# Block 0 of an adaLN transformer layer: three banks for exponentials, q and k sums as undivided products, gates' dots in the start's task list

## Chip, core and metric

One core of one Trainium2 chip. The metric is the device time of one execution in microseconds; of several runs the median is given. Before: 2514.73 us, median of 3 runs (2514.54 to 2520.65).

## What is computed

One transformer layer over 2048 rows of 576, with 32 heads of 18 and an MLP of 4608, conditioned on one vector `c`:

```python
mod = (silu(c) @ w_mod).reshape(1, 6, 1, 576)
sa, ca, ga, sb, cb, gb = (mod[:, i] for i in range(6))
h = layernorm(x) * (1 + ca) + sa
q, k, v = heads(h @ wqkv)                    # 32 heads of 18
x = x + ga * (softmax(q @ k.T * 18**-0.5) @ v) @ wo
h = layernorm(x) * (1 + cb) + sb
x = x + gb * (silu(h @ w1) @ w2)
```

All arrays are float32. Sums over the model's 576 columns are taken in three passes over a high and a low part of each operand (`PASS`: 14 products for 4 full and one folded group of 128 rows).

## The kernel before

**Stages.** The start (`start_tasks`) normalises all rows, transposes them into `hTh` and `hTl` (high and low part), takes the sums of k and q for the first columns and of all values, and stores them in DRAM (`kscr`, `qscr`, `vscr`). Attention then runs over 4 blocks of 512 query rows with 8 quads of 4 heads each. In block 0 the rest of the q and k sums is filled in between; in blocks 1 to 3 the output projection and the MLP of the block before are the filling, and block 3's MLP stands at the end.

**A slot of attention.** `slot_a` takes scores of queries against 512 keys (54 rows of the array, names `psa`) and VectorE their maximum (`mx`, `L670`). 38 slots later `slot_b` takes the same scores transposed, with the maxima in two further rows (56 rows of the array, `psb`), and ScalarE their exponential into `pt` (`L727`). Two heads sit in rows 0 to 63 and 64 to 127 of the array, so two score products run side by side: one pair is one psa and one psb product. When the four exponentials of a key tile are there, `pv` takes its values' run (`psv<-pt,vt`, `L762`): four heads in four groups of 32 columns. After 16 key tiles `out_b` transposes the quad's output (`pso`) and divides it. `max_b` transposes the maxima (`pst`) and writes them into rows of `qt` by DMA.

**Order.** TensorE's order is written at build time. For the start, `Start` plays a list of tasks with costs, dependencies, priorities and rings of buffers. For attention, a loop asks a model of VectorE and ScalarE (`Plan`, with a ring of banks for each PSUM pool) whether scores (`s`), a values' run (`v`) or filling (`f`) comes next. `Filler` holds the filling in order. The other engines' order is the scheduler's, except in the start's task list. An instruction that is recorded after the start can be drawn forward into it: the gates' loads are.

**PSUM.** Eight banks: `psB` 2 (scores for exponentials, `b`), `psF` 2 (sums, `f`), `psV` 1 (values, `v`), `psA` 3 (scores for maxima, and small transposes, `a`). `open_mlp`, called when the q and k sums are done, gives `psF` 3 and `psA` 2 for the rest.

**q and k sums in block 0** (`add_qk`, `qk_pair`). Twelve pairs of 512 columns. A pair takes both `psF` banks; `Pair.step` issues two products of 64 rows side by side, one for each bank, 28 steps in all; at half time the banks change their halves, behind an empty ScalarE instruction (`change`, `L470`) that the next products wait for. A product of 64 rows is in the same form of the array as the scores.

**Gates.** `mod_load` loads a column piece of `w_mod` (`wmt<-in_wcol`, `L491`), takes its dot with `sbc` on VectorE (`dot`, `L487`) and scales the identity by it (`dg`); `mod_piece` spreads it over the rows (`psm`). There are ten pieces, called from the filling of block 0. The start's task list has ten dots of its own (`wcl`, for the second modulation).

**Next weights.** `qk_load` loads a step's weights on ScalarE's queue (`raw<-in_wqkv`, `L512`), copies the high part on ScalarE (`wqh`, `L517`) and takes the low part on GpSimd (`L522`). Step 0's load stands in the start's task list.

Of the kernel before, what the change touches and what calls it, by code (L numbers as in the profile page):

```python
# [18 lines left out]
P = 128  # L19
# [6 lines left out]
KT = 5  # L26
# [23 lines left out]
XTB = 7  # L50
ETB = 3
# [14 lines left out]
NG = len(GR)  # L66
G2 = [range(i, i + 3) for i in range(0, 24, 3)]
# [7 lines left out]
EARLY_SLOTS = 16  # L75
KEEP = 6
NEAR = 500
LOADED = 900
STAND = 0
# [102 lines left out]
class Start:  # L182
# [3 lines left out]
    RATE = 300e3  # L186
# [16 lines left out]
    def ready(self, t):  # L203

        at = 0.0
        for d in t.deps:
            if d.end is None:
                return None
            at = max(at, d.end + (2.0 if d.eng == "D" else 0.0) + (self.LAG.get((d.eng, t.eng), 0.08) if d.eng != t.eng else 0.0) + t.lag)
# [12 lines left out]

    def run(self):
# [3 lines left out]
        while todo:  # L227
# [14 lines left out]
            for e, (_, t) in best.items():  # L242
# [10 lines left out]
                for k in t.free:  # L253
                    k.left -= 1
                    k.at = max(k.at, t.end + (2.0 if e == "D" else 0.0))
# [74 lines left out]
def tile_adaln_block(ctx: ExitStack, tc: tile.TileContext, x, wqkv, wo, w1, w2, c, wfirst, wcol, out):  # L330
# [9 lines left out]
    psF = ps0.enter_context(tc.tile_pool(name="psF1", bufs=2, space=PSUM))  # L340
# [76 lines left out]

    def bank_need():
# [70 lines left out]
    def mod_load(m, t):  # L489
        w = wqp.tile([P, D], F32, tag="wmt", name="wmt", bufs=2)  # L490
        nc.sync.dma_start(w, wcol[2 + m, :, t, :])  # L491
# [39 lines left out]
    def qk_load(which, m):  # L531
        raw = raw_load(qk_src(which, m), KT * P, nc.scalar)
# [3 lines left out]
    def qk_pair(which, m, ns, w, part):  # L536
        if part == 0:
            def ops(g, i):
                kt, a, b = PASS[i]
                return w[b][:, kt, :], (hTl if a else hTh)[:, kt, ns[g] * 512:(ns[g] + 1) * 512]  # L540
# [35 lines left out]
    state = {"now": 0, "p": 0, "k": 0, "tail": False, "tail2": False}  # L576
# [3 lines left out]
    def add_qk(steps):  # L580
        def load(i):
            which, m, _ = steps[i]
            fill.add(0, lambda: qk_w.update({i: qk_load(which, m)}))

        for i, (which, m, pairs) in enumerate(steps):
            for ns in pairs:
                names = [("qkx"[which], m, n) for n in ns]
                for p in range(NG):
                    fill.add(MMC * len(GR[p]), lambda i=i, which=which, m=m, ns=ns, p=p: qk_pair(which, m, ns, qk_w[i], p), name=names, need={0: pair_need, NG // 2: half_need}.get(p))
                    if ns == pairs[0] and p == 0 and i + 1 < len(steps):  # L590
                        load(i + 1)
                    if i >= MI and p in (NG // 2, NG - 1) and mods:
# [118 lines left out]
    def slot_b(s, j):  # L711
# [12 lines left out]
        ps = psB.tile([P, 512], F32, tag="b", name="psb", bufs=2)  # L724
# [69 lines left out]
    def open_mlp():  # L794
        nonlocal psF, psA
# [6 lines left out]
        plan.ring("f", 3)  # L802
        plan.ring("a", 2)
# [246 lines left out]
    def start_tasks(st):  # L1050
        S0 = Start({"b": 2, "f": 2, "v": 1, "a": 3, "xt": XTB, "wm": KT, "et": ETB, "vst": VSB, "qk": QKB, "raw": 2, "wq": 2})
# [78 lines left out]
        def T(g, kt):  # L1130
            d["T", g, kt] = psB.tile([P, 512], F32, tag="b", name="psT", bufs=2)
# [55 lines left out]
        def single(deps, ops, w, prio, key, free=()):  # L1187

            count[0] += 1
            ring = "v" if count[0] % 3 == 0 else "f"  # L1190
# [15 lines left out]
        def pair(deps, ops, w, n, prio, key, ring):  # L1206

            kb = tok(ring, 2)
            tasks = []

            def part(i):
                if i == 0:
                    ps = [(psF if ring == "f" else psB).tile([P, 512], F32, tag=ring, name="ps" + key[0], bufs=2)[:, :w] for _ in range(2)]
# [4 lines left out]
            for i in range(n):  # L1218
# [3 lines left out]
                tasks.append(add("P", (0.231 if w == 512 else 0.133) * 28 / n, lambda i=i: part(i), list(deps) + dep, prio, take=kb if i == 0 else ()))  # L1222
# [123 lines left out]
        for s in range(LEAD):  # L1346
# [6 lines left out]
            gate = h[3, KT - 1] if s >= EARLY_SLOTS else []  # L1353
# [10 lines left out]
        for n in range(2 * KT):  # L1364
# [10 lines left out]
        kr = tok("raw")  # L1375
        which, m, _ = steps[0]
        t = dma(328e3, lambda: d.update(rawn=raw_load(qk_src(which, m), KT * P, nc.sync)), prio=11, take=kr)
        kw = tok("wq")
        t = add("A", 0.74, lambda: d.update(whn=hi_part(d["rawn"])), [t], 11, take=kw)
        add("G", 1.54, lambda: qk_w.update({0: (d["whn"], lo_part(d["rawn"], d["whn"]))}), [t], 11, free=kr)  # L1380
# [12 lines left out]
    plan.ring("f", 2)  # L1393
    plan.ring("a", 3)
    plan.ring("b", 2)
# [23 lines left out]
    while now < 2 * (total + LEAD) or pend or later:  # L1419
# [17 lines left out]
        elif not mp:  # L1437

            if scores and ahead < AHEAD:
# [94 lines left out]
```

## Time and profile before

| | us |
|---|---|
| runs | 2520.65, 2514.54, 2514.73 |
| profiled execution, and its span | 2518.77, 2516.9 |
| first transpose on TensorE | 25.81 |
| first score product for a maximum | 63.72 |
| first exponential | 175.32 |
| last product of q and k sums | 564.6 |
| first output copy of block 0, and the last | 229.9, 613.1 |
| TensorE busy in 176 to 566 us | 385.15 of 390.00 |
| VectorE, ScalarE, GpSimd there | 312.88, 272.71, 10.94 |

Times of single instructions are from the span's start. A matmul's end is modelled, so TensorE's busy time also covers part of a wait; distances from one start to the next tell its pace. "PEld" is the weight load of a product, "SPq" and "ACTq" the issue of a DMA from SyncE's and ScalarE's queue, "ACTq L470" the empty instruction of `change`.

### The profile page before, as it was taken

The page shows a single profiled execution, that of the slowest core. Times are in us where ns is not written, and L with a number is a line of the kernel's source. Part 1 is how long each engine was busy: PE and PEld are TensorE (multiplying, and loading weights), DVE is VectorE, ACT ScalarE, POOL GpSimd, SP SyncE. Part 2 cuts the span into 40 slices and gives each one's busy share as a digit, 9 for nine tenths or more (in the row PEclk, how much of TensorE's full clock was granted, in tenths as well). Part 3 has the DMA queues.
Part 4 walks back from the last instruction along what each step waited for, and adds up shares of the span by engine and source line. Part 5 has one row for each costly group of instructions (what it writes and reads, how often), then busy time and mean ns, then how long its engine had stood idle before and what let it go on. Part 6 is the DMA issues. An engine that isn't in the chain of part 4 may idle for free.

```text
span 2516.9 us, 51969 instructions
## 1 busy us (share of the span) xinstructions
PE 2422.2 (96%) x20528; PEld 1617.7 (64%) x20528; DVE 1783.0 (71%) x3180; ACT 1498.0 (60%) x2712; POOL 577.1 (23%) x729
## 2 busy tenths in 40 slices
PE   4989999998999999999999999999999999999999
PEld 3874444542556666666666666666666666678988
DVE  6867878887786777777877777777877777324333
ACT  3326776776566666666576766666666666642121
POOL 3300000003375566654211111111211111110000
PEclk9999999999899999999999999999999999999999
DMA  7653233235265555554443433334543334226563
GB/s 244 200 170 120 93 107 102 88 111 180 78 202 173 166 170 189 191 162 162 160 145 125 145 119 135 121 123 131 181 146 126 126 134 142 102 95 235 171 222 122
DMA packets 159397, 372.07 MB, mean 148 GB/s; under 512 B 17754, under 2 KB 55034, under 8 KB 159154
## 3 DMA queue, kind: packets, MB, share of 16 engines
q1 hardware_dynamic: 153906, 366.12, 43.9%
q8 instruction: 163, 2.67, 0.4%
q10 hardware_dynamic: 5248, 2.62, 0.4%
q14 instruction: 80, 0.66, 0.1%
HBM read 282.35 MB, written 85.80 MB: 146 GB/s over the span
## 4 chain that ended last, share of the span: by engine, by line
PE 86%; DVE 7%; ACT 2%; DMA 2%; issue 1%; POOL 1%; SPq 0%; ACTq 0%; DVEq 0%; POOLq 0%
PE ps L459 26%; PE psv L762 18%; PE psa L668 14%; PE ps L453 9%; PE psb L725 9%; PE psqk L459 3%; DVE mx L670 3%; PE psp L459 1%; PE psv L459 1%; ACT pt L727 1%; PE pso L775 1%; PE psv L1199 1%; PE psqk L1199 1%; PE psp L453 1%; DVE st L368 1%
## 5 line engine op out<-in xcount | busy, mean ns | idle before, releaser
L670 DVE TENSOR_REDUCE mx<-psa 128x1 f32<-128x512 f32 x2048 | 1346.3, 687 | 387.4 <-PE psb L725 256.8
L727 ACT ACTIVATE pt<-psb 128x512 f32<-128x512 f32 x2048 | 1169.6, 597 | 569.9 <-PE psb L725 397.4
L725 PE MATMUL psb<-qt,kt 56*128 56x512 f32 x2048 | 817.2, 433 | 12.3 <-DMA qt<-mt 5.9
L668 PE MATMUL psa<-kt,qt 54*128 54x512 f32 x2048 | 780.2, 421 | 27.8 <-DVE mx L670 21.3
L668 PEld LDWEIGHTS psa<-kt,qt 54*128 54x128 f32 x2048 | 348.8, 185 | 393.1 <-DVE mx L670 247.3
L762 PE MATMUL psv<-pt,vt 128*32 128x512 f32 x4096 | 534.6, 606 | 0.8 <-DMA vt<-vscr 0.8
L459 PE MATMUL ps<-w2t,g 64*128 64x288 f32 x4992 | 418.1, 294 | 0.1
L459 PEld LDWEIGHTS ps<-w2t,g 64*128 64x128 f32 x4992 | 387.1, 185 | 35.1 <-issue 10.6
L725 PEld LDWEIGHTS psb<-qt,kt 56*128 56x128 f32 x2048 | 352.6, 185 | 78.9 <-ACT pt L727 58.4
L459 PE MATMUL ps<-hh,w1t 64*128 64x512 f32 x2160 | 386.2, 395 | 0.9 <-POOL hh L401 0.8
L459 PEld LDWEIGHTS ps<-hh,w1t 64*128 64x128 f32 x2160 | 221.7, 186 | 57.4 <-issue 10.6
L978 POOL TENSOR_TENSOR g<-etmp,g 128x512 fp32r<-128x512 f32 x108 | 138.9, 1302 | 405.8 <-ACT g L977 362.7
L883 POOL TENSOR_TENSOR x<-x,gt 128x288 f32<-128x288 f32 x116 | 92.7, 800 | 483.1 <-ACT gt L882 473.1
L762 PEld LDWEIGHTS psv<-pt,vt 128*32 128x32 f32 x4096 | 93.1, 108 | 171.4 <-issue 164.6
L459 PE MATMUL ps<-hl,w1t 64*128 64x512 f32 x864 | 186.7, 393 | 1.0 <-POOL hl L399 1.0
L879 DVE TENSOR_TENSOR x<-ps,x 128x288 f32<-128x288 f32 x184 | 84.0, 456 | 122.6 <-PE ps L453 71.5
L453 PE MATMUL ps<-w2t,g 128*128 128x288 f32 x960 | 130.6, 295 | 1.7 <-ACT g L977 0.9
L453 PEld LDWEIGHTS ps<-w2t,g 128*128 128x128 f32 x960 | 128.6, 188 | 3.3 <-ACT g L977 1.2
L974 ACT ACTIVATE eq<-ps 128x512 f32<-128x512 f32 x36 | 21.5, 598 | 146.4 <-PE ps L453 146.4
L453 PE MATMUL ps<-hh,w1t 128*128 128x512 f32 x360 | 106.9, 390 | 0.5 <-DVE hh L401 0.5
L522 POOL TENSOR_TENSOR wql<-raw,wqh 128x640 fp32r<-128x640 f32 x13 | 21.3, 1640 | 366.8 <-ACT wqh L517 340.0
L459 PEld LDWEIGHTS ps<-hl,w1t 64*128 64x128 f32 x864 | 94.0, 186 | 17.5 <-POOL hl L399 2.5
(136 smaller groups left out, 2085.5 us busy)
## 6 DMA issues: line engine op xcount, KB each, us to landing
w1t<-w1s SPq DMA_DIRECT2D x108, 640.0 KB
w2t<-w2s SPq DMA_DIRECT2D x108, 576.0 KB
kt<-kscr SPq DMA_DIRECT2D x512, 108.0 KB
w1s<-w1t SPq DMA_DIRECT2D x36, 640.0 KB
w2s<-w2t SPq DMA_DIRECT2D x36, 576.0 KB
vt<-vscr SPq DMA_DIRECT2D x32, 608.0 KB
qt<-qscr SPq DMA_DIRECT2D x128, 108.0 KB
raw<-in_w SPq DMA_DIRECT2D x72, 160.0 KB
```

The lines of the kernel that those rows point to most:

```text
L368: nc.vector.bn_stats(st6[:, j, :], src[:, j * HH:(j + 1) * HH])
L453: mm(self.ps[late], lhsT=lhsT, rhs=rhs, start=(i == 0), stop=(i == self.n - 1))
L459: done = mm(self.ps[g], lhsT=lhsT[rows], rhs=rhs[rows], start=(s == 0), stop=(s == 2 * self.n - 1))
L668: mm(ps, lhsT=t["q"][64 * j:64 * j + 54, hp, stt * P:(stt + 1) * P], rhs=t["k", kc, hp][64 * j:64 * j + 54, :], start=True, stop=True)
L670: return lambda: nc.vector.tensor_reduce(t["mx"][:, 2 * j + hp, stt, kc:kc + 1], ps, axis=AX.X, op=ALU.max)
L725: mm(ps, lhsT=t["k", kt // 4, hp][64 * e:64 * e + 56, kt % 4 * P:(kt % 4 + 1) * P], rhs=t["q"][64 * e:64 * e + 56, hp, :], start=True, sto ...
L727: nc.scalar.activation(t["P"][kt, hp][:, e, :], ps, AF.Exp, scale=SCALE)
L762: mm(t["ps"][32 * h:32 * h + 32, :], lhsT=t["v"][:, c0:c0 + 32], rhs=t["P"][kt, h // 2][:, h % 2, :], start=(kt == 0), stop=(kt == NKT - 1 ...
L879: nc.vector.tensor_add(c["x1"][j][:, hs], ps, c["x1"][j][:, hs])
L883: nc.gpsimd.tensor_add(c["x1"][j][:, hs], c["x1"][j][:, hs], t)
L978: (nc.vector if last else nc.gpsimd).tensor_tensor(g[:, 1, :], t, f(g[:, 0, :]), op=ALU.subtract)
L1199: mm(d["s", key][:, :w], lhsT=lhsT, rhs=rhs, start=(i == 0), stop=(i == 13))
```

## The change

- PSUM in block 0: `psB` 2 and a new pool `psX` 1 for exponentials (`bank_b` takes them in turn), `psF` 1. In the start, sums take `psF` and `psV` in turn.
- q and k sums of block 0: one bank of 512 columns at a time, 14 products of 128 rows in four parts (`qk_one`, `GQ`), marked as the full form of the array. In the loop a new first choice takes filling when the model's array isn't in the form of halves and VectorE has 900 ns of work waiting.
- Gates: `mod_load` keeps the scaling of the identity; the ten loads and dots become tasks of the start with the ten others, all after row group 3's first transposed piece (before: the ten after group 2's).
- Next weights: steps 0 and 1 are both loaded from SyncE's queue by tasks of the start.
- The start: 8 row tiles for 7, 4 temporary tiles for 3, other rates in the model; scores for maxima wait in the model for group 2 (before: the first 16 slots free, later ones for group 3), pairs of sums on `b` for group 3.

```diff
-XTB = 7
-ETB = 3
+XTB = 8
+ETB = 4
+GQ = (range(0, 4), range(4, 8), range(8, 11), range(11, 14))
+LOADED2 = 900
+NEXT = 8
-    RATE = 300e3
+    RATE = 320e3
+    LANDING = 3.0
...
-    psF = ps0.enter_context(tc.tile_pool(name="psF1", bufs=2, space=PSUM))
+    psF = ps0.enter_context(tc.tile_pool(name="psF1", bufs=1, space=PSUM))
+    psX = ps0.enter_context(tc.tile_pool(name="psX", bufs=1, space=PSUM))
...
+    def bank_b(name):
+
+        state["b"] += 1
+        if psX is not None and state["b"] % 3 == 0:
+            return psX.tile([P, 512], F32, tag="x", name=name)
+        return psB.tile([P, 512], F32, tag="b", name=name, bufs=2)
...
     def mod_load(m, t):
-        w = wqp.tile([P, D], F32, tag="wmt", name="wmt", bufs=2)
-        nc.sync.dma_start(w, wcol[2 + m, :, t, :])
-        g = gcol[:, m, t:t + 1]
-        dot(w, g)
         dg = wqp.tile([P, P], F32, tag="dg", name="dg", bufs=1)
-        nc.vector.tensor_scalar(dg, ident, g, 1.0 if m == 0 else 0.5, op0=ALU.mult, op1=ALU.mult)
+        nc.vector.tensor_scalar(dg, ident, gcol[:, m, t:t + 1], 1.0 if m == 0 else 0.5, op0=ALU.mult, op1=ALU.mult)
...
-    def qk_pair(which, m, ns, w, part):
+    def qk_one(which, m, n, w, part):
         if part == 0:
...
-            qk_ps[0] = Pair([psF.tile([P, 512], F32, tag="f", name="psqk") for _ in ns], ops, 14, True)
-        for s in GR[part]:
-            qk_ps[0].step(s)
-        if part == NG - 1:
-            for g in range(2):
-                qk_out(which, m, ns[g], qk_ps[0].ps[g])
-                chain([("A", 600), ("V", 690)], plan.t + 200, None, qk_ps[0].release[g])
+            qk_ps[0] = psF.tile([P, 512], F32, tag="f", name="psqk")
+            qk_ps[1] = plan.take("f")
+        for i in GQ[part]:
+            kt, a, b = PASS[i]
+            mm(qk_ps[0], lhsT=w[b][:, kt, :], rhs=(hTl if a else hTh)[:, kt, n * 512:(n + 1) * 512], start=(i == 0), stop=(i == 13))
+        if part == len(GQ) - 1:
+            qk_out(which, m, n, qk_ps[0])
+            chain([("A", 600), ("V", 690)], plan.t + 200, None, qk_ps[1])
...
-        ps = psB.tile([P, 512], F32, tag="b", name="psb", bufs=2)
+        ps = bank_b("psb")
...
-            gate = h[3, KT - 1] if s >= EARLY_SLOTS else []
+            gate = h[2, KT - 1]
...
-        for n in range(2 * KT):
+        for n in range(4 * KT):
...
-            t = dma(295e3, col_load, h[2, 0], 12, take=k)
-            add("V", 0.95, lambda m=m, t_=t_: mod_dot(2 + m, t_, d["wc", m, t_]), [t], 12, free=k)
+            t = dma(295e3, col_load, h[3, 0], 12, take=k)
+            add("V", 0.95 if m < 2 else 0.83, col_dot, [t], 12, free=k)
...
+        for i, (which, m, _) in enumerate(steps[:2]):
...
-    plan.ring("f", 2)
+    plan.ring("f", 1)
-    plan.ring("b", 2)
+    plan.ring("b", 3)
...
-            if scores and ahead < AHEAD:
+            if busy and plan.mode != "half" and ahead > -NEXT and plan.backlog("V") >= LOADED2:
+                do = "f"
+            elif scores and ahead < AHEAD:
                 do = "s"
```

TensorE in block 0, in the first quad, from one values' run on. Before (two runs of sums between the scores are half products, two side by side):

```order
L762 MATMUL psv_2152<-pt_2070,vt_2074 32x512 x2
L762 MATMUL psv_2152<-pt_2071,vt_2074 32x512 x2
L668 MATMUL psa<-kt_89,qt 128x512
L725 MATMUL psb<-qt,kt_80 128x512
L668 MATMUL psa<-kt_89,qt 128x512
L725 MATMUL psb<-qt,kt_80 128x512
L459 MATMUL psqk<-hTh,wqh 128x512 x2
L459 MATMUL psqk<-hTh,wql 128x512 x2
L668 MATMUL psa<-kt_90,qt 128x512
L725 MATMUL psb<-qt,kt_79 128x512
```

The same stretch after (`L551` is the undivided product of `qk_one`):

```order
L768 MATMUL psv_2184<-pt_2103,vt_2109 32x512 x2
L768 MATMUL psv_2184<-pt_2104,vt_2109 32x512 x2
L674 MATMUL psa<-kt_92,qt 128x512
L731 MATMUL psb<-qt,kt_83 128x512
L674 MATMUL psa<-kt_92,qt 128x512
L731 MATMUL psb<-qt,kt_82 128x512
L674 MATMUL psa<-kt_92,qt 128x512
L731 MATMUL psb<-qt,kt_82 128x512
L551 MATMUL psqk<-hTl,wqh 128x512
L551 MATMUL psqk<-hTh,wqh 128x512
L551 MATMUL psqk<-hTh,wql 128x512
L674 MATMUL psa<-kt_92,qt 128x512
```

Three pairs of scores now follow a values' run before the sums, where two did, and the sums are three undivided products in a row between scores. Over the stretch from the first pair of scores to the last product of sums the rows before have 460 psb products, 114 values' runs, 672 half products in 143 runs, and the array goes 23 times from halves to the full form and 9 times back; after, 457, 114, 336 undivided products in 89 runs, 99 times and 85 times. 11 borders of a products' run after are with a values' run. From five pairs of scores behind the last product on, TensorE's rows are the same.

SyncE's queue in the start, up to the first load of q (`qt`). Before:

```order
L642 DMA kt_78<-kscr 54x512 x2
L491 DMA wmt<-in_wcol 128x576
L566 DMA qscr<-qkhl 128x512
L568 DMA qscr<-qkhl 128x2x512
L1265 DMA vscr<-vst_126 128x4x152
L491 DMA wmt<-in_wcol 128x576 x2
L632 DMA qt<-qscr 54x512 x4
```

After:

```order
L572 DMA qscr<-qkhl 128x512
L574 DMA qscr<-qkhl 128x2x512
L648 DMA kt_82<-kscr 54x512 x2
L648 DMA kt_83<-kscr 54x512 x2
L638 DMA qt<-qscr 54x512 x4
L572 DMA qscr<-qkhl 128x512
L574 DMA qscr<-qkhl 128x2x512
L1379 DMA wcl<-in_wcol 128x576 x4
```

The gates' loads ahead of the q load are gone; column loads now begin behind it, and two k tiles stand ahead of it.

VectorE in the start, before (row statistics of group 0, then the factors that its rows wait for):

```order
L1118 TENSOR_SCALAR t_223<-t_223 128x4
L487 SCALAR_TENSOR_TENSOR wmt,gcol<-wmt,sbc 128x576
L1119 TENSOR_TENSOR rs<-r_210,t_223 128x4
L487 SCALAR_TENSOR_TENSOR wmt,gcol<-wmt,sbc 128x576
L495 TENSOR_SCALAR dg<-ident,gcol 128x128
L1120 SCALAR_TENSOR_TENSOR nm<-mv,rs 128x4
```

After, among the maxima:

```order
L676 TENSOR_REDUCE mx<-psa 128x1 x2
L498 SCALAR_TENSOR_TENSOR wcl,gcol<-wcl,sbc 128x576
L502 TENSOR_SCALAR dg<-ident,gcol 128x128
L676 TENSOR_REDUCE mx<-psa 128x1 x2
L498 SCALAR_TENSOR_TENSOR wcl,gcol<-wcl,sbc 128x576
```

The gates' dots have moved from the row factors' chain to between pairs of maxima.

More of the change, by code (lines that the diff above doesn't have):

```diff
@@ L208, in ready @@
                 return None
-            at = max(at, d.end + (2.0 if d.eng == "D" else 0.0) + (self.LAG.get((d.eng, t.eng), 0.08) if d.eng != t.eng else 0.0) + t.lag)
+            at = max(at, d.end + (self.LANDING if d.eng == "D" else 0.0) + (self.LAG.get((d.eng, t.eng), 0.08) if d.eng != t.eng else 0.0) + t.lag)
         n = {}
@@ L254, in run @@
                     k.left -= 1
-                    k.at = max(k.at, t.end + (2.0 if e == "D" else 0.0))
+                    k.at = max(k.at, t.end + (self.LANDING if e == "D" else 0.0))
                 t.fn()
@@ L582, in load @@
             which, m, _ = steps[i]
-            fill.add(0, lambda: qk_w.update({i: qk_load(which, m)}))
+            fill.add(0, lambda: qk_w.update({i: qk_load(which, m, i)}))
         for i, (which, m, pairs) in enumerate(steps):
[L586 to L590, printed above, removed]
+            for n in sum(pairs, ()):
+                names = [("qkx"[which], m, n)]
+                for p in range(len(GQ)):
+                    fill.add(MMC * len(GQ[p]), lambda i=i, which=which, m=m, n=n, p=p: qk_one(which, m, n, qk_w[i], p), name=names, need=bank_need if p == 0 else None, mode="full")
+                    if n == pairs[0][0] and p == 0 and i + 1 < len(steps):
                         load(i + 1)
-                    if i >= MI and p in (NG // 2, NG - 1) and mods:
+                    if i >= MI and p == len(GQ) - 1 and mods:
                         mt_ = mods.pop(0)
@@ L1050, in start_tasks @@
     def start_tasks(st):
-        S0 = Start({"b": 2, "f": 2, "v": 1, "a": 3, "xt": XTB, "wm": KT, "et": ETB, "vst": VSB, "qk": QKB, "raw": 2, "wq": 2})
+        S0 = Start({"b": 3, "f": 1, "v": 1, "a": 3, "xt": XTB, "wm": KT, "et": ETB, "vst": VSB, "qk": QKB, "raw": 2, "wq": 2})
         add, dma = S0.add, S0.dma
@@ L1130, in T @@
         def T(g, kt):
-            d["T", g, kt] = psB.tile([P, 512], F32, tag="b", name="psT", bufs=2)
+            d["T", g, kt] = bank_b("psT")
             for j in range(4):
@@ L1189, in single @@
             count[0] += 1
-            ring = "v" if count[0] % 3 == 0 else "f"
+            ring = "fv"[count[0] % 2]
             kb = tok(ring)
@@ L1206, in pair @@
         def pair(deps, ops, w, n, prio, key, ring):
-            kb = tok(ring, 2)
+            kb = tok(ring, 2) if ring == "b" else tok("f") + tok("v")
             tasks = []
@@ L1212, in part @@
                 if i == 0:
-                    ps = [(psF if ring == "f" else psB).tile([P, 512], F32, tag=ring, name="ps" + key[0], bufs=2)[:, :w] for _ in range(2)]
+                    ps = [(bank_b("ps" + key[0]) if ring == "b" else p_.tile([P, 512], F32, tag="fv"[j], name="ps" + key[0]))[:, :w] for j, p_ in enumerate((psF, psV))]
                     d["s", key] = Pair(ps, ops, 14, True, False)
@@ L1221, in pair @@
                     dep = [add("A", 0.03, lambda: d["s", key].change(), dep, 0)]
-                tasks.append(add("P", (0.231 if w == 512 else 0.133) * 28 / n, lambda i=i: part(i), list(deps) + dep, prio, take=kb if i == 0 else ()))
+                gate = h[3, KT - 1] if ring == "b" else []
+                tasks.append(add("P", (0.231 if w == 512 else 0.133) * 28 / n, lambda i=i: part(i), list(deps) + gate + dep, prio, take=kb if i == 0 else ()))
             return kb, tasks[-1]
@@ L1370, in col_load, with col_dot @@
                 nc.sync.dma_start(d["wc", m, t_], wcol[m, :, t_, :])
-            t = dma(295e3, col_load, h[2, 0], 12, take=k)
-            add("V", 0.95, lambda m=m, t_=t_: mod_dot(2 + m, t_, d["wc", m, t_]), [t], 12, free=k)
[L1375 to L1380, printed above, removed]
+            def col_dot(m=m, t_=t_):
+                if m < 2:
+                    mod_dot(2 + m, t_, d["wc", m, t_])
+                else:
+                    dot(d["wc", m, t_], gcol[:, m - 2, t_:t_ + 1])
+            t = dma(295e3, col_load, h[3, 0], 12, take=k)
+            add("V", 0.95 if m < 2 else 0.83, col_dot, [t], 12, free=k)
+        for i, (which, m, _) in enumerate(steps[:2]):
+            kr, kw = tok("raw"), tok("wq")
+            t = dma(328e3, lambda i=i, src=qk_src(which, m): d.update({("rn", i): raw_load(src, KT * P, nc.sync)}), prio=11, take=kr)
+            if i == 0:
+                t = add("A", 0.74, lambda: d.update(whn=hi_part(d["rn", 0])), [t], 11, take=kw)
+                add("G", 1.54, lambda: qk_w.update({0: (d["whn"], lo_part(d["rn", 0], d["whn"]))}), [t], 11, free=kr)
+            else:
+                qk_raw[1] = lambda: d["rn", 1]
         S0.run()
```

15 lines of the change are left out of this document (7 added, 8 removed).

## Prediction

> **What bounds the kernel now.** I read the page's head first, then the busy time of one stretch, then who waits for whom in it, and last the order of time on single engines. The span falls into a start (0 to 176 us), the part of block 0 in which the remaining q and k sums are taken (176 to 566 us), a short rest of block 0, and blocks 1 to 3 with the MLP. The change touches the first two.
>
> ```profile
> span 2516.9 us, 51969 instructions
> PE 2422.2 (96%) x20528; PEld 1617.7 (64%) x20528; DVE 1783.0 (71%) x3180; ACT 1498.0 (60%) x2712; POOL 577.1 (23%) x729
> ...
> 176.00:566.00 390.00, 385.15 (x2548) 192.02 (x2550) 312.88 (x551) 272.71 (x507) 10.94 (x7) 1.00 0.33 104
> ...
> L459 PE MATMUL psqk<-hTh,wql x300: 383/393/502, 116.8 to 564.6; 64*128 64x512 f32 x150
> ```
>
> By the second line TensorE (PE) is busy 96% of the span, and 385 of 390 us in block 0's stretch (columns of the third row: PE, PEld, DVE, ACT, POOL, granted clock, DMA share, GB/s); the last row has the last sum product at 564.6. Were that work, 390 us could not shrink without less work. The order of time in that stretch says otherwise:
>
> ```profile
> 250.32 1.06 PE L762 MATMUL psv<-pt,vt 128*32 128x512 f32 x8
> 251.32 0.50 PE L668 MATMUL psa<-kt,qt 54*128 54x512 f32 x1
> ...
> 251.90 0.40 PE L668 MATMUL psa<-kt,qt 54*128 54x512 f32 x1
> 252.54 0.49 PE L725 MATMUL psb<-qt,kt 56*128 56x512 f32 x1 [0.25 <-ACT pt L727]
> ...
> 253.03 0.50 PE L725 MATMUL psb<-qt,kt 56*128 56x512 f32 x1
> 253.46 1.07 PE L762 MATMUL psv<-pt,vt 128*32 128x512 f32 x8
> ...
> 262.86 1.07 PE L762 MATMUL psv<-pt,vt 128*32 128x512 f32 x8
> ...
> 264.43 0.40 PE L459 MATMUL psqk<-hTh,wqh 64*128 64x512 f32 x2
> 264.67 0.40 PE L459 MATMUL psqk<-hTh,wql 64*128 64x512 f32 x2
> ...
> 265.99 1.07 PE L762 MATMUL psv<-pt,vt 128*32 128x512 f32 x8
> ...
> 269.33 1.07 PE L762 MATMUL psv<-pt,vt 128*32 128x512 f32 x8
> ```
>
> From one values' run to the next lies one key tile: four pairs of scores (psa for the maxima, psb for the exponentials). With no sum product the cycle is 3.14 us (250.32 to 253.46), with two steps of q and k sums 3.13 (262.86 to 265.99), with four 3.34 (265.99 to 269.33). A step issues in 0.24 us (264.43 to 264.67), yet the first two cost nothing. So PE is not the bound: a cycle needs four pairs at 0.23, the values' run of 1.00 (250.32 to 251.32) and 0.20 to get into it (253.03 to 253.46 less 0.23), 2.12 in all, and idles 1.0 without sums, 0.54 with two steps, 0.28 with four. What it waits for is seen at 252.54: the third psb has its maxima partner ready at 251.90, but both psb banks are held until an exponential ends.
>
> ```profile
> ACT pt L727 <- PE psb L725: 72.2, 87, 1.7
> PEld psa L668 <- DVE mx L670: 70.2, 84, 1.1
> ...
> PEld psb L725 <- ACT pt L727: 43.3, 164, 2.4
> ...
> L670 DVE TENSOR_REDUCE mx<-psa 128x1 f32<-128x512 f32 x457 | 290.1, 685 | 76.8 <-PE psb L725 48.6 <-PE psa L668 25.0
> ...
> 129.82 1.29 DVE L670 TENSOR_REDUCE mx<-psa 128x1 f32<-128x512 f32 x2
> ```
>
> These are the waits (us in total, times, longest) and the maxima's group of 176 to 566 us, and from the start two maxima back to back: 1.29 for both, so one each 0.60. ACT and VectorE (DVE) wait for scores, the scores wait for banks: a loop through two banks, 164 times. DVE works 313 of 390 us, so it has 77 us of room.
>
> **The change, block 0.** Between the first pair and the last sum product the order before has 460 pairs, 114 values' runs, 672 half products (336 steps) and 24 short runs of transposes and gate products. PE needs 460 x 0.23 = 106, 114 x 1.20 = 137, 336 x 0.23 = 77, and about 12 for the short runs (an estimate, 0.5 each with their changes): 332 of 390. Idle is 58. Cycle by cycle it is the same: 62 cycles with two steps x 0.54, 42 with four x 0.28 and 7 without x 1.0 make 52.
>
> The order after keeps pairs and values' runs and has 336 products of 128 rows in 89 runs. It does not put them next to the values' runs: 11 borders of a products' run touch one, the rest stand between scores of 64 rows, as the order's rows show. Each such run pays two changes of the array's form, which half products never did. Their price is in the start, where both forms stand side by side:
>
> ```profile
> 76.50 0.39 PE L1199 MATMUL psqk<-hTh,wql 128*128 128x512 f32 x1
> 76.82 0.50 PE L668 MATMUL psa<-kt,qt 54*128 54x512 f32 x2
> 77.25 0.53 PE L1199 MATMUL psv<-wv,hTh 128*128 128x288 f32 x2
> ```
>
> From full to half 0.32 less 0.23 = 0.09; from half to full 0.43 less 0.23 = 0.20. The order counts 76 more changes each way: 76 x 0.29 = 22 us added to PE. The Trainium skill (TensorEngine Tiling (Array Packing), Key Properties) says that changing the tiling mode, not just the tile, drains the array; by that rule alone the edit loses its 22 us, and the trace's 0.29 per round trip agrees that the drain is real.
>
> Against it stands the third bank. In the cycle without sums the third psb would go at 251.90 and not 252.54; the fourth then waits for what the third waits for now, and the values' run comes some 0.5 earlier. In cycles with products the fourth pair comes after the products' run (0.20 + 3 x 0.23 + 0.09, about 1 us), by when the first exponential has ended, so 0.54 and 0.28 go to about nothing. What stays: the quads' joints (58 less 52 = 6) and 6 cycles of four straight pairs at 0.5, 9 us, and half as much again because DVE now runs fuller (457 maxima start 0.6 apart, plus 39 of other work, is 313 of 370): I take 15. Bounds: none of the idle goes (58 stay, +22) or all goes (-36). I take 58 - 15 - 22 = **-21 us**, near the cycle rows. One bank for sums instead of two: a column's first product waits for the ACT copy and DVE difference of the column before, which the order covers with scores; their price is in the 15. Fewer, undivided sums also need no turn of halves on ACT. After the last product both orders are the same for 18 key tiles, and so is the MLP; I cost that at nothing.
>
> **The change, start.** Here PE stands still twice, and each time runs slowly afterwards:
>
> ```profile
> 63.72 1.28 PE L668 MATMUL psa<-kt,qt 54*128 54x512 f32 x2 [3.56 <-DMA qt<-qscr]
> ...
> 69.81 0.63 PE L1199 MATMUL psqk<-hTh,wqh 128*128 128x512 f32 x1
> 70.24 0.63 PE L1199 MATMUL psqk<-hTh,wql 128*128 128x512 f32 x1
> ...
> 72.64 0.40 PE L1199 MATMUL psqk<-hTh,wql 128*128 128x512 f32 x1
> ...
> 146.16 0.85 PE L459 MATMUL psv<-wv,hTh 64*128 64x288 f32 x4 [4.91 <-ACTq L470]
> ...
> 148.49 0.68 PE L459 MATMUL psv<-wv,hTh 64*128 64x288 f32 x4
> ...
> 149.21 0.68 PE L459 MATMUL psv<-wv,hTh 64*128 64x288 f32 x4
> ...
> 55.67 3.60 SPq L491 DMA_DIRECT2D wmt<-in_wcol  x2
> 60.01 1.38 SPq L632 DMA_DIRECT2D qt<-qscr  x4
> ...
> 61.69 0.76 DVE L487 SCALAR_TENSOR_TENSOR wmt<-wmt,sbc 128x576 f32<-128x576 f32 x1 [2.79 <-DMA wmt<-in_wcol]
> ...
> 63.17 0.76 DVE L395 CAST hTh<-etmp 128x512 fp32r<-128x512 f32 x2
> ...
> 142.47 0.55 ACTq L512 DMA_DIRECT2D raw<-in_wqkv  x1
> ...
> 143.12 0.74 ACT L517 ACTIVATE wqh<-raw 128x640 fp32r<-128x640 f32 x1 [7.17 <-DMA qt<-qscr]
> ...
> 175.32 3.18 ACT L727 ACTIVATE pt<-psb 128x512 f32<-128x512 f32 x5 [2.57 <-DMA vscr<-vst]
> ...
> 65.00:130.00 65.00, 65.00 (x481) 54.03 (x480) 57.07 (x120) 24.67 (x42) 18.19 (x21) 0.94 0.65 203
> 130.00:200.00 70.00, 62.24 (x617) 47.13 (x613) 45.00 (x74) 25.42 (x50) 3.27 (x4) 0.95 0.49 160
> ```
>
> The first stop: the scheduler drew the gates' column loads (wmt) to the front. SP stood on two of them from 55.67, and the first q load behind them (60.01) went out late; DVE waited 2.79 for one, with a cast of the transposed rows behind it. The change puts these ten loads and dots last in the task list, and in the new order no gate load stands ahead of the q load. Gone: 3.6 us, and the slow stretch behind it (0.43 per product, 69.81 to 70.24, not 0.23; over the 8.9 us to 72.64, when the short rows are back, about 4 us are lost). The second stop: ACT stood 7.17 us, by the profile for q loads, with a weight load's issue (142.47) in its queue, and the copies of the sums and a turn of halves behind it were late. The new order has one ACT load less there, since SP fetches the first two, and a values' sum under way while the turn is waited for: I take the 4.9 and its slow stretch (0.72 for six halves from 148.49 to 149.21; at half the first one's length, 2.2) as gone but for 2. The granted clock is 0.94 and 0.95 in the two windows around them (the last rows, columns as above) against 1.00 in block 0. The Trainium skill (TensorE: Matmul & The Clock Gate, What's actually happening) gives the cause: an idle window of about 3.4 us halves the array's clock. The 0.43 behind a 3.56 us gap agrees.
>
> Added: all twenty dots now stand among the start's maxima, 10 x 0.76 = 7.6 us on DVE more than before. From the first maximum to the end PE has about 74 us of products by the order, DVE 77 maxima x 0.60 + 20 dots x 0.76 + 8 differences of q and k at about the same 0.6 = 66: covered on average, and where two dots stand close PE waits; I take 3. Eight row tiles instead of seven let group 1's rows in early, against its transposes standing ahead of other products: 0 (-2 to +3). Ten loads queue on SP behind the q loads: 0, nothing needed soon follows. Sum: 14.7 - 2 - 3, rounded up for the rest I may not see: **-12 us** (bounds -18 and +5).
>
> **Sum.** -21 - 12 = -33. The profiled execution took 2518.77 (span 2516.9, 1.9 around it), 4.0 above the median of 2514.73; 2485.8 for the like of it, **2481.7** against the median. Under 0.3% (7.5 us) a measurement cannot tell a change from none.
>
> **Rivals.** *Drains decide, slower.* Scores now come in bursts of five pairs and then a products' run; if DVE's and ACT's latencies refill the idle that the bank frees, PE gains nothing and pays 22. For it: 70.2 us of waits are for maxima, whose three banks don't change. Against: the maxima's waits follow the missing psb partner. It tips over when more than 48 of the 58 us of idle remain; with all of it and the start's gain, 2514.7 + 22 - 12 = 2525. 12%.
> *Bank and drain cancel,* 22 regained and 22 paid: only the start gains, 2503. 15%.
> *The start gains nothing* because dots and maxima now collide, or the ACT load stalls again and halves the clock; block 0 as forecast: 2494. 10%.
> *Everything goes:* idle to nothing (-36) and the whole start (-15): 2464. 8%.
> My forecast, with its own range 2470 to 2493, 55%. All but the first are faster, part of the second within 0.3%: faster 0.82, same 0.06, slower 0.12. The range from 2462 to 2508 leaves out the first rival and little else.
>
> **What would show it.** Right: cycles of about 3.0 us in place of 3.13 and 3.34; psb waits for ACT well under 164; last sum product near 532 us and not 564.6; first exponential near 163 and not at 175.32; no PE gap over 3 us and full clock before them. Wrong: cycles above 3.3 with 89 runs each 0.29 longer than their products, waits for maxima above 70 us, or a new gap at the first q load or behind ACT's weight loads.

## The result, and the profile after

Four runs of each kernel: 2492.14 us for the changed one (2489.13 to 2495.11), 2516.87 for the one before. The ratio is 0.9893, with a 95% interval from 0.988 to 0.9907: about 27 us faster (the medians are 25 apart), where I had forecast 33. The time lies at the upper edge of my range, 2470 to 2493. Both kernels were run and profiled once more later (2487.35 for the changed one beside 2517.2, ratio 0.9878, interval 0.9864 to 0.9891; the second profile of before comes from a later run of that kernel), so that what repeats can be told from what does not:

| us in the profiled execution | before | again | changed | again |
|---|---|---|---|---|
| span | 2516.9 | 2513.7 | 2490.2 | 2487.5 |
| first psb product | 171.80 | 169.12 | 162.17 | 159.93 |
| first exponential | 175.32 | 172.64 | 165.69 | 163.45 |
| last product of q and k sums | 564.62 | 563.61 | 541.29 | 536.73 |
| transposes of block 0's last output (pso) | 624.7 | 623.7 | 602.5 | 600.4 |
| the same of block 1's first quad | 692.4 | 688.4 | 664.6 | 662.4 |

Between the first profiles the 26.7 us fall so: 9.6 up to the first exponential, 13.7 in the stretch of the sums, 1.1 given back up to block 0's end, 5.6 gained in block 1's first quad, 1.1 given back behind it. Between the second ones 26.2: 9.2, 17.7, 3.6 given back, 2.7 gained, and 0.2 gained behind it.

Part of the gain is TensorE's clock. Its granted mean was 0.991 and 0.993 in the profiles of before and 0.996 in both of the changed kernel. A spell at half rate loses at most half its length; added up behind the first transpose that is 22.4 and 17.1 us before, 9.1 and 8.9 changed, so at most 13 and 8 of the 26 us. It lies in the start and in block 1's first quad; in the stretch of the sums it is 0 and 3.4 us before, 3.4 and 1.7 changed.

The head of the page of the changed kernel, three stretches of it (columns as in the prediction: PE, PEld, DVE, ACT, POOL, granted clock, DMA share, GB/s), and the last group of sum products:

```profile
span 2490.2 us, 51321 instructions
PE 2399.7 (96%) x20192; PEld 1574.5 (63%) x20192; DVE 1787.7 (72%) x3180; ACT 1490.4 (60%) x2712; POOL 577.9 (23%) x729
```

```profile
65.00:130.00 65.00, 62.66 (x517) 52.93 (x516) 54.94 (x103) 14.68 (x29) 11.65 (x8) 0.98 0.82 267
130.00:166.00 36.00, 35.13 (x446) 32.24 (x442) 23.82 (x44) 6.01 (x17) 0.15 (x2) 0.99 0.41 126
166.00:541.00 375.00, 368.99 (x2200) 153.64 (x2201) 310.77 (x549) 263.47 (x504) 10.90 (x7) 0.99 0.35 110
```

```profile
L551 PE MATMUL psqk<-hTh,wql x120: 388/397/632, 163.3 to 541.3; 128*128 128x512 f32 x120
```

PE's busy share says as little as before (96%). The clock in the start has risen from 0.94 and 0.95 to 0.98 and 0.99. In the stretch DVE now works 311 of 375 us. Who waits for whom there (us in total, times, longest):

```profile
PEld psa L674 <- DVE mx L676: 99.0, 143, 1.7
ACT pt L733 <- PE psb L731: 86.1, 130, 2.8
...
DVE mx L676 <- PE psb L731: 45.8, 85, 2.5
...
PEld psb L731 <- ACT pt L733: 3.2, 4, 1.6
```

The wait for an exponential's bank has gone from 164 times to 4. The wait for a maximum's bank has grown from 84 times and 70.2 us to 143 and 99.0: it is what TensorE meets next. In the order of time, from one values' run over a run of sums to the next two:

```profile
305.12 1.07 PE L768 MATMUL psv<-pt,vt 128*32 128x512 f32 x8
306.12 0.49 PE L674 MATMUL psa<-kt,qt 54*128 54x512 f32 x1
...
306.69 0.40 PE L731 MATMUL psb<-qt,kt 56*128 56x512 f32 x1
307.02 0.49 PE L551 MATMUL psqk<-hTl,wqh 128*128 128x512 f32 x1
307.35 0.39 PE L551 MATMUL psqk<-hTh,wqh 128*128 128x512 f32 x1
307.58 0.39 PE L551 MATMUL psqk<-hTh,wql 128*128 128x512 f32 x1
307.90 0.50 PE L674 MATMUL psa<-kt,qt 54*128 54x512 f32 x1
...
308.57 1.07 PE L768 MATMUL psv<-pt,vt 128*32 128x512 f32 x8
...
310.23 1.07 PE L768 MATMUL psv<-pt,vt 128*32 128x512 f32 x8
```

The change of the array's form is seen at 306.69 to 307.02 (0.33, of which 0.10 is the change), 307.02 to 307.35 (0.33, 0.10) and 307.58 to 307.90 (0.32, 0.09): 0.29 for a round trip, as the start had shown. Two values' runs, seven pairs and three products take 5.11 us (305.12 to 310.23); by the prediction's prices they need 2 x 1.20 + 7 x 0.23 + 3 x 0.23 + 0.29 = 4.99. This part of the order has hardly any idle time left.

The first stop of the start is gone: from 40 to 90 us no two neighbouring products of the changed kernel's profiles start more than 1.3 us apart, where before the longest distance was 3.8 and 3.5. The second is shorter but there. In the order of time, engines mixed:

```profile
121.75 5.09 SPq L638 DMA_DIRECT2D qt<-qscr  x7
...
126.17 0.64 ACTq L519 DMA_DIRECT2D raw<-in_wqkv  x1
126.86 0.74 ACT L524 ACTIVATE wqh<-raw 128x640 fp32r<-128x640 f32 x1 [7.11 <-DMA qscr<-qkhl]
127.11 0.50 PEld L470 LDWEIGHTS psv<-wv,hTh 64*128 64x128 f32 x4 [2.17 <-ACTq L481]
127.11 0.85 PE L470 MATMUL psv<-wv,hTh 64*128 64x288 f32 x4 [1.84 <-ACTq L481]
```

ACTq L481 is `change`, the empty instruction at the turn of halves. It stands behind a weight load's issue (126.17), which ScalarE reaches only while SyncE issues the second q load: the scheduler has drawn the load of step 2 forward into the start, where before it had drawn another.

### The profile page after: what moved, and what is told of

The parts are those of the page before. It is cut to its first block, busy times and chain, and to the rows that moved or that the text cites. A ratio compares the mean times of both kernels' runs of the same rounds, so it can differ in the third digit from the quotient of the medians.

```text
span 2490.2 us, 51321 instructions
## 1 busy us (share of the span) xinstructions
PE 2399.7 (96%) x20192; PEld 1574.5 (63%) x20192; DVE 1787.7 (72%) x3180; ACT 1490.4 (60%) x2712; POOL 577.9 (23%) x729
## 4 chain that ended last, share of the span: by engine, by line
PE 86%; DVE 7%; DMA 2%; ACT 2%; POOL 1%; issue 1%; SPq 1%; ACTq 0%; DVEq 0%; POOLq 0%
PE ps L470 26%; PE psv L768 19%; PE psa L674 14%; PE ps L464 10%; PE psb L731 8%; DVE mx L676 4%; PE psqk L551 3%; PE psp L470 1%; PE psv L470 1%; PE pso L781 1%; DVE etmp L983 1%; DMA xt<-in_x 1%; PE psp L464 1%; ACT pt L733 1%; ACT etmp L982 1%
## 5 line engine op out<-in xcount | busy, mean ns | idle before, releaser
L674 PE MATMUL psa<-kt,qt 54*128 54x512 f32 x2048 | 770.4, 424 | 26.9 <-DVE mx L676 22.7
L731 PE MATMUL psb<-qt,kt 56*128 56x512 f32 x2048 | 787.8, 428 | 8.5 <-DMA qt<-mt 5.1
L731 PEld LDWEIGHTS psb<-qt,kt 56*128 56x128 f32 x2048 | 347.3, 185 | 39.1 <-ACT pt L733 18.4
L529 POOL TENSOR_TENSOR wql<-raw,wqh 128x640 fp32r<-128x640 f32 x13 | 20.7, 1589 | 372.6 <-PE psa L674 112.0
```

Of the source, the lines that this page charges most:

```text
L674: mm(ps, lhsT=t["q"][64 * j:64 * j + 54, hp, stt * P:(stt + 1) * P], rhs=t["k", kc, hp][64 * j:64 * j + 54, :], start=True, stop=True)
L731: mm(ps, lhsT=t["k", kt // 4, hp][64 * e:64 * e + 56, kt % 4 * P:(kt % 4 + 1) * P], rhs=t["q"][64 * e:64 * e + 56, hp, :], start=True, sto ...
```

## The experiments

Ratios are to the kernel before, timed beside. Two measures are used: how long TensorE has stood or run slowly since its first transpose (time less the products issued, at 0.231 us for 512 rows, 0.133 for 288, 0.125 for a transpose, half of the product's price for half products, 0.117 for a score), called standing time; and block 0 from its first exponential to its last quad's transposes, which does not depend on where an order puts the last product of sums (before 449.4 and 451.1, changed 436.8 and 437.0).

**The start alone.** The changed kernel with `psF` 2, `psB` 2 and `qk_pair` again:

```diff
-    psF = ps0.enter_context(tc.tile_pool(name="psF1", bufs=1, space=PSUM))
-    psX = ps0.enter_context(tc.tile_pool(name="psX", bufs=1, space=PSUM))
+    psF = ps0.enter_context(tc.tile_pool(name="psF1", bufs=2, space=PSUM))
...
-            if busy and plan.mode != "half" and ahead > -NEXT and plan.backlog("V") >= LOADED2:
-                do = "f"
-            elif scores and ahead < AHEAD:
+            if scores and ahead < AHEAD:
```

> The changed start, with block 0 as in the kernel before (two banks for exponentials, two for sums, half products). My theory: the start's gain is its own, so the first psb product comes near 162 us as in the changed kernel (before 171.8), and block 0 from there takes its 389 us again: 2516.9 less 9.6, about 2507 us; about 2502 if the half-clock spell at the opening of block 1 is also short. Rival, the start's gain is only handed on to a wait in block 0 (the first exponential waits for values or k tiles all the same): 2515 to 2517.

2514.45 us, ratio 0.9987 (0.9977 to 0.9997): a third of the gain expected. The row of its second stop tells why:

```profile
140.08 0.85 PE L465 MATMUL psv<-wv,hTh 64*128 64x288 f32 x4 [7.08 <-ACTq L476]
```

TensorE had stood 9.8 us at 125 us, against 20.5 and 17.5 before: the gates' stop was gone. Then the wait behind a weight load's issue held it for 7.1 us, and it ran at half rate after it: 12.7 us up to the first psb product, against 7.7 and 8.1 before. Block 0 took 453.3 us, some 3 more than before, with 3.4 us at half rate lost in 240 to 255 us that neither profile of before has there (the second has as much at 173 to 180 us). The step that fell is "the start's gain is its own".

**Block 0 alone.** Banks, sums and rule as changed; `mod_load`, the ten tasks, the weights' loads and the start's sizes as before:

```diff
-XTB = 8
-ETB = 4
+XTB = 7
+ETB = 3
...
-        for n in range(4 * KT):
+        for n in range(2 * KT):
```

> Banks, undivided sums and the loop's new rule as in the changed kernel; gates' dots, next weights, tiles and gates of the start as before. My theory: the stretch from the first exponential to the last product of sums takes 375 us as in the changed kernel (before 389), the start its old time: about 2503 us, 2497 if the spell at the opening of block 1 is short. Rival, part of the 14 us came from the loads that the start took out of block 0 (gates' dots on VectorE, two weight loads on ScalarE's queue): stretch 380 or more and 2508 or above.

2503.81 us, ratio 0.9946 (0.9933 to 0.9958), and 373.7 us from first exponential to last product. As expected: block 0 gains its part without the start. 14 and 3 us make 17, not 27. By the profiles the halves lack the rest in the start and in block 0: in the start alone the second stop cost 12.7 us, against 5.8 in the whole, and block 0 took some 3 more than before; here TensorE had stood 24.7 us ahead of its second stop, against 20.7 and 17.6 before (why was not tried). Block 1's first quad adds nothing to it: 62.8 us here, 62.0 in the whole.

**Undivided sums without the third bank.** `psF` 2, `psB` 2, the rest as changed, with 96 runs of sums for 89:

```diff
-    plan.ring("f", 1)
+    plan.ring("f", 2)
     plan.ring("a", 3)
-    plan.ring("b", 3)
+    plan.ring("b", 2)
```

> As the changed kernel, but two banks for exponentials and two for sums; sums stay undivided products of 128 rows. My theory, the third bank is what removed the idle time and the undivided form only costs (0.29 us a run): the psb banks are waited for again some 100 times or more, stretch 389 us or longer, about 2507 us or above. Rival, runs of three or four undivided products by themselves give ScalarE the time to empty its two banks: psb waits stay under 50 and the stretch under 380 us, 2492 to 2497.

2526.98 us, ratio 1.0045 (1.0031 to 1.006); 407.4 us from first exponential to last product, 18 and 16 more than before; 472.0 for block 0, 23 and 21 more. The undivided form alone costs a little less than its 96 further changes each way at 0.29 would (28 us), and the third bank takes 32 us off it (407.4 to 375.6; about 30 without the spells at half rate). The loop's new rule stands in both kernels; it was not tried by itself.

```profile
PEld psa L669 <- DVE mx L671: 106.2, 167, 1.0
...
PEld psb L726 <- ACT pt L728: 30.6, 53, 0.8
PE psb L726 <- ACT pt L728: 10.2, 40, 0.3
```

The waits for exponentials' banks are back: 93 times, 41 us, over both kinds of row (by the same count 178 times and 48 us in the kernel before, 5 and 4 in the changed one).

**The bank given to the maxima.** `psA` 4, `psB` 2, one for sums:

```diff
-    plan.ring("a", 3)
-    plan.ring("b", 3)
+    plan.ring("a", 4)
+    plan.ring("b", 2)
```

> As the changed kernel, but the freed bank goes to the maxima: four psa banks, two psb, one for sums. My theory, the exponentials' bank was the short one: psb waits return (over 100), psa waits fall far below 143, stretch 385 us or longer, 2502 or above. Rival, after the change the maxima's banks (99 us of waits) are the limit and any third bank would have done: stretch 375 or shorter, 2492 or below.

2533.16 us, ratio 1.0065 (1.0052 to 1.0078); 405.9 us. The exponentials' bank was the short one: the last experiment, with the same 96 runs of sums, had given the freed bank to the sums, and giving it to the maxima is 1.5 us better by this measure. But the psa waits did not fall as I had expected (144 times, 95.7 us):

```profile
PEld psa L669 <- DVE mx L671: 95.7, 144, 1.2
...
PEld psb L726 <- ACT pt L728: 29.1, 49, 2.2
PE psb L726 <- ACT pt L728: 11.1, 33, 1.8
```

They are 167 times and 106.2 us in the last experiment, so most of them are not for want of a fourth bank. That VectorE itself is late at them, after scores have come in bursts, fits this but is not shown apart.

**Runs of seven, runs of two.**

```diff
-GQ = (range(0, 4), range(4, 8), range(8, 11), range(11, 14))
+GQ = (range(0, 7), range(7, 14))
```

> As the changed kernel, but a sum's 14 products stand in two parts of seven, not four of four or three: 48 runs in place of 89, and 32 to 34 changes of the array's form fewer each way. By the price of a change (0.29 us a round trip) block 0 loses 9 to 10 us: stretch from first exponential to last product 366 in place of 375.6, about 2483 us. Rival, a run of seven (1.6 us and its changes) is longer than the banks' scores keep VectorE and ScalarE busy, TensorE waits for maxima afterwards, and nothing is won or some is lost: 2490 to 2500.

2502.55 us, ratio 0.9937 (0.9924 to 0.9949): 10 to 15 slower than the changed kernel, not 9 faster. Block 0 takes 448.5 us for 437, though 33 round trips of 0.29 are saved:

```profile
PEld psa L674 <- DVE mx L676: 119.9, 179, 1.1
```

The rival held: nothing is won, and the waits for maxima have grown from 143 times and 99.0 us. I read it so that a long run leaves the scores' banks idle, and the pairs behind it come faster than VectorE takes their maxima. With two products a part (111 runs), on the kernel of the next-but-one experiment:

> As sums_two_banks_in_start (2484.0 us), but sums in parts of two products: 111 runs in place of 89, the array changes its form 10 times more into full and 23 more back to halves. Theory, the changes cost 0.29 a round trip and nothing else moves: stretch from first exponential to last product 5 us longer, 2489 us. Rival, what limits is the burst of maxima around a products' run (99 us of waits for psa, 120 with runs of seven): shorter runs spread the scores, psa waits fall under 85 us, and the stretch is 3 to 8 us shorter: 2476 to 2481.

2492.01 us, ratio 0.9899 (0.9883 to 0.9915), 8 slower than the kernel it was built on; block 0 takes 440.4 us for 435.2, which is the price of 10 and 23 further changes (about 5 us). Up to the last product of sums it takes 13.5 us longer and not 5, but this order has ten more pairs of scores ahead of that product. The psa waits do not fall (168 times, 103.5 us). Between 48 and 111 runs the 89 of the change are the best of the three.

**Next weights by SyncE.**

```diff
-        raw = qk_raw.pop(i)() if i in qk_raw else raw_load(qk_src(which, m), KT * P, nc.scalar)
+        raw = qk_raw.pop(i)() if i in qk_raw else raw_load(qk_src(which, m), KT * P, nc.sync)
```

> As the changed kernel, but the next weights' loads that still stand on ScalarE's queue (two of them in the start, behind the first wqh copy) go out on SyncE's queue, behind the second q load. My theory, the second stop is ScalarE standing at the issue of that load, with the empty instruction of the turn of halves behind it: the stop at 124.9 us (2.2 us in the changed kernel, then half rate to 134 us, 4.8 together) goes, first psb product near 157.4 in place of 162.17, about 2487 us. Rival, ScalarE waits for the data of the copy itself or for a store, and the stop stays wherever the load is issued: 2491 to 2493.

The stop is gone. ScalarE's two copies of weights now stand at 118 and 123 us, the second waiting, by the profile, for products of sums and not behind a load's issue, and the load goes out at 126.31 on SyncE while TensorE goes on:

```profile
118.08 0.74 ACT L524 ACTIVATE wqh<-raw 128x640 fp32r<-128x640 f32 x1 [2.50 <-PE psqk L470]
123.00 0.74 ACT L524 ACTIVATE wqh<-raw 128x640 fp32r<-128x640 f32 x1 [4.18 <-PE psqk L470]
```

```profile
120.19 5.70 SPq L638 DMA_DIRECT2D qt<-qscr  x8
126.31 0.55 SPq L519 DMA_DIRECT2D raw<-in_wqkv  x1
```

The first psb product comes at 157.74, and block 0 ends 7.7 us earlier than in the changed kernel's first profile, 5.6 earlier than in its second. The time, 2486.89 us (0.9879, 0.9866 to 0.9893), is 5 under the changed kernel's first measurement and the same as its second: 4.3 of the 7.7 us were lost again in block 1's first quad. That the stop is the load's issue on ScalarE is shown; that the kernel gains by removing it is not. What the issue itself waits for was not tried.

**Two sums banks in the start.** As the last, and the start's sums take `psF` and the third bank in turn:

```diff
+        def bank_f(name):
+            fcount[0] += 1
+            return (psF if fcount[0] % 2 else psX).tile([P, 512], F32, tag="xf"[fcount[0] % 2], name=name)
```

> As weights_by_sync, and in the start the third bank of the exponentials serves the sums (two psqk banks and psv, two banks for transposes), as in the kernel before; from the first exponential on it is the third psb bank. My theory, one sums bank costs the start 3.9 us (TensorE stood 13.7 us up to 125 us in the changed kernel, 9.8 with two sums banks) and the second stop, 7 us and its slow spell with two sums banks, is ScalarE's load issue and goes: first psb product near 153.5, about 2483 us. Rival, the work that waits in the start's tail (transfers of the second quad's k and q, values' stores) ends when it ended and the first exponential stays at 160 or later: 2489 to 2492.

2484.01 us, ratio 0.9862 (0.9847 to 0.9878). First psb product at 156.22, not 153.5: TensorE had stood 12.4 us at 125 us, where one sums bank gives 12.8 (the last experiment). The first psb product comes 1.5 us earlier than there, 0.6 of it ahead of the first transpose. One bank for sums costs the start at most 1.5 us and not 3.9; the rest of the difference to the start alone would be its order, which was not tried. This is the fastest kernel measured, but its interval overlaps that of the changed kernel's second measurement, so it is not shown to be faster.

**Gates back.** The gates' loads and dots recorded in the filling again, with 7 row tiles and 3 temporary ones as before the change:

```diff
     def mod_load(m, t):
+        w = wqp.tile([P, D], F32, tag="wmt", name="wmt", bufs=2)
+        nc.sync.dma_start(w, wcol[2 + m, :, t, :])
+        g = gcol[:, m, t:t + 1]
+        dot(w, g)
```

> As the changed kernel, but the ten gates' loads and dots are left to the scheduler again, as before the change, with 7 row tiles and 3 temporary tiles to make room for them. My theory, they stand ahead of the first q load again and cost what the first stop cost, 8 us with its half-rate spell, less the 1 us that the late dots cost: first psb product near 169, about 2499 us. Rival, the first stop came of the old group order and not of the gates: 2490 to 2494.

2505.5 us, ratio 0.9951 (0.9938 to 0.9963). TensorE had stood 22.9 us at 125 us, 9 more than in the changed kernel; the second stop was 7.3 us here and the first psb product at 178.40, where I had expected 169. Of the 16 us behind the changed kernel 9.6 fall up to the second stop, 5 at it, and 1.6 ahead of the first transpose. That the gates, with the tiles set back beside them, cost the start so much up to the second stop is shown; the expectation had nothing for the second stop, which grew as well. The gates' loads stand among SyncE's first stores again, the first q load comes behind them, and DVE waits for them:

```profile
43.51 0.34 SPq L502 DMA_DIRECT2D wmt<-in_wcol  x1
44.40 0.40 SPq L578 DMA_DIRECT2D kscr<-qkhl  x1
45.59 0.34 SPq L502 DMA_DIRECT2D wmt<-in_wcol  x1
...
66.95 2.06 SPq L642 DMA_DIRECT2D qt<-qscr  x4
```

```profile
DVE wmt L498 <- DMA wmt<-in_wcol: 6.2, 4, 2.1
```

**Half products with the third bank.** Three `b`, two `f`, two `a`:

```diff
-    plan.ring("f", 1)
-    plan.ring("a", 3)
+    plan.ring("f", 2)
+    plan.ring("a", 2)
```

> The third bank for exponentials with half products: three psb, two psqk, two psa, one psv; start as in the changed kernel, with two banks for sums. It asks whether the sums had to become undivided. Theory, the bank for exponentials is what counts and a maxima bank little (the fourth one brought 1.5 us): no changes of form to pay (26 us), stretch about 350 to 365 us, 2480 to 2490. Rival, with two banks for maxima the loop through VectorE (a score, 0.6 us of maximum, a bank) becomes what TensorE waits for: over 200 waits for psa, stretch 390 or longer, 2515 or above.

2569.61 us, ratio 1.0208 (1.0193 to 1.0223). Block 0 takes 496.0 us. My theory was far off: a fourth bank for maxima had brought next to nothing, but going from three to two costs block 0 45 to 47 us net of what the third bank for exponentials brings, more than the whole change gains.

```profile
PEld psa L677 <- DVE mx L679: 169.5, 290, 2.1
```

With eight banks the third one for exponentials could only come out of the sums, and the undivided form was the price of that.

**The two kernels again.**

> The changed kernel once more, to see what repeats. Start and block 0 should repeat within 1 to 2 us (first psb product 162, last product of sums 541), and the time 2489 to 2495. Open: the half-rate spell at the opening of block 1, which lost 10 us in the profile of before, 1.7 in that of the changed kernel and 2 to 10 in the others, all with the same rows there. Theory A, it varies from one execution to the next: another loss than 1.7 us here. Theory B, it is set by the kernel: 1.7 again.

> The kernel before once more. In its first profile the opening of block 1 lost 10.0 us of full rate (670 to 690 us) and the stop behind ScalarE's load issue was 4.9 us; in the changed kernel the opening lost 1.7 in both profiles, the stop was 2.2 and 1.5. Theory A, these belong to the kernel: 9 to 11 us at the opening again, a stop of 4 to 6 us. Theory B, they vary from one execution to the next: the opening loses under 6 us or the stop is off by more than 1.5 us, and of the 26.7 us between the two profiles so much was chance.

The changed kernel gave 2487.35 us, the kernel before 2516.54 (ratio to itself 0.9995, 0.9983 to 1.0007). At block 1's opening the changed kernel lost 1.7 us of full rate again, the kernel before 5.1 and not 10.2. From the last product ahead of the second stop to the next it was 1.45 us in the changed kernel (2.23 in its first profile), 5.24 in the kernel before (5.30). So the stop belongs to the kernel, and of the loss at the opening some 5 us are chance.

## Why the prediction was right, and where it was not

**What bounds.** Right. That TensorE's 96% hid a loop through two banks is shown by the third bank: 32 us with the sums' form the same, and 164 waits become 4.

**Block 0: -21, measured -13.7 and -17.7.** Most of the spread is the clock: without the spells at half rate the stretch takes 389.3 and 387.6 us before and 372.2 and 371.6 changed, which is 17.1 and 16.0. The price of a change held (0.29, in place at 306.69 to 307.90, and by the runs of two). Undivided sums on two banks lost 16 to 23 us by the two measures, for 28 by that price, so the 22 us are of the right size and no more than that is shown. The mis-sized term is the idle time that stays. Six kernels with this order take 371.8 to 375.6 us (mean 373.4) where the sum needs 332 + 22 = 354: 19 us stay, not 15, 1 to 2 of them half rate. I had added half again for a fuller DVE; the psa waits rose by 29 us, and the sign that I named for "wrong", waits for maxima above 70 us, came true beside the signs for "right". The first rival's mechanism did act, then, but far below the 48 us of idle at which it decides. The runs of seven show the same limit from the other side. The last product stood at 541.3 and 536.7, where I had said 532. Cycles "of about 3.0 us" did not come as one kind: 1.7 with two pairs, 3.45 with five and three products; per four pairs that is 2.9. That is one good place: over the whole stretch, with its 114 values' runs, a key tile takes 3.41 and 3.43 us before, 3.29 and 3.27 changed.

**Start: -12, measured -9.6 and -9.2.** The working gave 14.7 - 2 - 3 = 9.7, and 9.6 and 9.2 were measured (0.6 and 0.9 of it ahead of the first transpose, where I had nothing); "rounded up for the rest I may not see" was the error. Within it two terms were off against each other. The first stop and the late dots together brought 7.0 and 4.0 us up to the second stop (I had 7.6 less 3). The second stop kept 5.8 and 3.7 us of 7.7 and 8.1, where I had let 2 stay of 7.1: "one ACT load less there" was no reason, since the scheduler drew another load to the same place. So the second stop gave 1.9 and 4.4 us for my 5.1, and in the first pair of profiles the 9.6 came out by luck, a term too large beside one too small; in the second pair both are within 0.7. A gap behind ScalarE's weight loads was one of my signs for "wrong", and it came, 2.23 and 1.45 us long from product to product. The run with the loads on SyncE shows that this stop was to be had by the queue, not by the number of loads.

**After the sums: nothing, measured -3.4 and +0.7** from the last product on, from the pieces listed with the table. I had counted the rows, which are the same, and not the clock on them.

**The rivals.** Drains did not decide; bank and drain do not cancel (32 against 18); the start gained; not everything went. The forecast's own case came, short by 4 us in block 0 and by 2 in the start.

## What to carry to other kernels

Where an engine is "busy" 96% but its cycle is longer than its work, look for the ring that it goes round and count its buffers: one bank moved from a user that can do with one to a user that stands at two was worth 32 us, while a fourth bank next door brought 1.5 us and the loss of the third there cost about 45. A change of the array's form can be priced from two rows and counted from the order, but fewer runs were not better here: with longer ones the waits for maxima grew by more than the changes saved. A load's issue that the scheduler had put into ScalarE's queue stopped TensorE through it: with one such instruction removed the next one came in, and only the change of queue took the stop away, though no measurable time was gained.

## What the runs showed of the hardware

The granted clock fell to half without any idle stretch near 3 us. Stretches of 3.42 us ahead of such spells and the spells themselves (columns as above, the granted clock third from the end), in the changed kernel at the first exponentials and at block 1's opening:

```profile
164.64:168.06 3.42, 2.57 (x9) 1.25 (x9) 1.63 (x3) 2.37 (x5) 0.15 (x2) 1.00 0.52 131
168.06:171.48 3.42, 3.42 (x15) 1.04 (x13) 1.64 (x3) 1.77 (x4) 0.00 (x0) 0.50 0.68 278
649.34:652.76 3.42, 1.78 (x11) 0.84 (x9) 3.10 (x10) 1.68 (x3) 2.99 (x6) 1.00 0.46 169
652.76:656.18 3.42, 3.35 (x14) 0.70 (x12) 2.13 (x5) 0.96 (x2) 2.25 (x5) 0.50 0.13 36
```

At the same opening in the kernel before (first profile), and with the weights by SyncE:

```profile
666.34:669.76 3.42, 2.06 (x14) 0.56 (x6) 3.42 (x7) 1.73 (x4) 3.34 (x5) 1.00 0.74 219
669.76:690.24 20.48, 19.23 (x71) 7.72 (x69) 12.49 (x27) 11.25 (x18) 10.25 (x16) 0.50 0.46 155
```

```profile
641.92:645.34 3.42, 1.76 (x13) 0.79 (x15) 3.13 (x9) 1.68 (x3) 3.31 (x6) 1.00 0.38 136
645.34:659.00 13.66, 13.30 (x50) 5.87 (x45) 7.86 (x15) 8.38 (x13) 7.00 (x10) 0.50 0.46 146
```

Ahead of each spell TensorE is busy for 1.8 to 2.6 of 3.42 us, with no distance over 1.5 us between two products. The spells last 3.42, 3.42, 20.48 and 13.66 us: one, one, six and four times the same length, and each loses half of it, 1.7 us, where TensorE has work. The Trainium skill (TensorE: Matmul & The Clock Gate, What's actually happening) gives a free-running window of about 3.4 us, and half rate after an idle one. The lengths agree with the window; here windows that were half to three quarters busy were enough. Where a stretch has many short waits, the same rows can so cost 1.7 us or 10, and of one kernel 10 in one execution and 5 in the next; what sets the number of windows was not tried. The second stop is the other face of it: in the kernel before 5.3 us without a product cost 7.7 with the half rate behind it, in the start alone 7.6 us cost 12.7.
